# A state-space scan feeding a gated MLP: the first block's set-up, its loads and its weight preparation are ordered anew

## The chip, the cores and the metric

The kernel runs on one core of one Trainium2 chip, as one program. The metric is the device time of one execution in microseconds (us). Before the change three runs took 351.63, 351.94 and 352.17 us; the median is 351.94 us.

## The reference, cut to what matters

```python
# x [4,8,768,32], a [4,8,768], B, C [4,8,768,16]: batch, heads, sequence, width
la, cum = log(clip(a, 1e-6, 1)), cumsum(la)            # within chunks of the sequence
M  = (C @ B.T) * exp(cum_i - cum_j) * causal
y  = M @ x + (C @ state) * exp(cum)                    # inside the chunk + carried in
state = exp(sum(la)) * state + sum_j(B_j x_j * exp(cum_last - cum_j))
x  = y.transpose(0, 2, 1, 3).reshape(3072, 256)        # tokens x model width
g, val = x @ w_gate, x @ w_val                         # 256 -> 1536
return (g * sigmoid(g) * val) @ w_out                  # 1536 -> 256
```

All inputs and outputs are 32-bit floats.

## The kernel before, in words

The sequence is cut into NB = 6 blocks of 128 positions. A block holds these positions of all four batches, 512 tokens, and goes through two stages: the scan (here called attention) and the MLP.

The scan of a block works on two pieces of 64 positions. VectorE (DVE) builds the decay tile `L` with a running product (`scan_spread` in block 0, `scan_j` later): it multiplies along a row of `a` and restarts at 1 wherever the tile `dj` holds a 1, that is on the diagonal of a piece. TensorE (PE) forms the scores `S` (`scores`), DVE multiplies them by `L` (`mix`) and the keys by the decay to the piece's end (`weigh_first` in block 0, `weigh_b` later), PE forms the piece states (`sums`), the outputs `y` (`values`) and the part carried in (`carried`). `E` is the second decay tile; `ce` names the product of C with it (`weigh_c`); `apart` and `step` advance the state.

In block 0 the rows of `a` are loaded small (`load_rows`), clipped on DVE (`clip_rows`) and spread over the partitions by matmuls with a 0/1 tile (`spread`); later blocks read them back from DRAM, clipped by GpSimd (POOL) and written there once (`clip_all`, `write_all`, then `load_aj` and `load_an`).

The MLP has NF = 12 pieces f of 128 hidden units. `gate_val` makes two 128x512 products per piece, ScalarE (ACT) applies `silu`, DVE multiplies (`product`). `hid_high` and `hid_low` split the result in a rounded high part and its rest, and `project` sums three products (high-high, low-high, high-low) over all pieces. `gate_val` does the same three products in blocks 1 to 5. In block 0 it multiplies the whole 32-bit floats instead, x in the tile `xf` and the weights in `w`, which needs no low parts.

The weights arrive as 64-bit words and are made into 32-bit floats on chip, 18 pieces in all: 12 for gate and value (`wg0` to `wg11`), 6 for the projection (`wo0` to `wo5`). Piece i goes through `w_fetch` (512 KB on SP's DMA queue), `w_magnitude` and `w_rest` on ACT, `w_range` (on DVE for pieces 1 and 2, on POOL for the others), `w_shift`, `w_sign` and `w_round` on DVE. A gate piece is then ready for block 0. For the later blocks `w_high` rounds it to the tile `h`, `w_minus` writes its negative, and `w_low` adds the whole in a DMA issued by POOL, which leaves the low part `l`.

The order is written by a planner. `Plan.add` takes an engine, a cost, the steps that must come before (`needs`), the slots that a step takes and a rank; `Plan.order` plays the kernel with these costs and writes each engine's instructions in the order that comes out. An engine then executes its instructions strictly in that order. `needs` and `Plan.follow` (a list of steps that go in turn) put no wait on the chip: waits come from the data alone, and from tiles that must be free again. `lag` is the time that the planner gives a transfer on a bus that all transfers share, `slack` a margin. Tiles come from pools with a number of buffers: raw weights have 8 (`RAW`), shared with the high and low parts of the hidden values; `sg` has 21, shared by gate weights `w` and hidden values; `L`, `E`, `bc` (B and C) and `xb` (x and B by position) have one each, so that the loads of block k+1 wait for the scan of block k.

## Time and profile before

| | us |
|---|---|
| three runs: lowest, median, highest | 351.63, 351.94, 352.17 |
| profiled execution, its own time | 352.14 |
| its span | 350.3 |

The profile is of one execution. Its span is the stretch from the first to the last instruction; 1.84 us of that execution's own time lie around it. Engines are PE (matmul), PEld (weight load), DVE, ACT, POOL and SP; SPq, ACTq and POOLq are their queues where they issue DMAs. A row of a timeline has start, duration, engine, operation, written tile <- read tiles, count, and in brackets the idle time of the engine before it with what ended it. Busy PE time is 342.8 us of 350.3; the granted TensorE clock is 9 tenths or more in all 40 slices of the span.

### The profile page before, as it was taken

Reading aid. Unit: us, or ns where it says so; the run is one execution under the profiler, and the core shown is the slowest. Engines: PE = TensorE matmul, PEld = TensorE weight load, DVE = VectorE, ACT = ScalarE, POOL = GpSimd, SP = SyncE. Lnnn points to the kernel's source line nnn. Section 1 sums busy time; section 2 is a strip of 40 time slices with the busy share of each in tenths; the row PEclk is TensorE's granted clock in tenths of the full one; section 3 lists DMA queues with packets and bytes.
Section 4 is the critical chain, followed back from the end, with each engine's and each line's share of the span. In section 5 each row is a group of like instructions: output and inputs, shape, how many; then the busy total and the mean of one; then the engine's idle time right before and its main releaser. Section 6 shows DMA issues by size and latency. Waiting matters only on the chain.

```text
span 350.3 us, 7386 instructions
## 1 busy us (share of the span) xinstructions
PE 342.8 (98%) x3183; PEld 265.6 (76%) x3184; DVE 231.3 (66%) x415; ACT 121.9 (35%) x221; POOL 46.0 (13%) x36
## 2 busy tenths in 40 slices
PE   7999989999999999999999999999999999999996
PEld 5644445688878888878888878888888888888895
DVE  4999999998689774686447677456676430565320
ACT  3599677434355512212222222221212221222221
POOL 1374884402301000000000000000000000000000
PEclk9999999999999999999999999999999999999999
DMA  7799998850000751000382000281000000100001
GB/s 258 241 318 309 334 277 185 225 120 2 1 2 4 204 158 62 0 2 2 111 175 82 0 2 2 84 199 59 24 3 2 2 2 0 60 2 0 0 2 60
DMA packets 10216, 31.28 MB, mean 89 GB/s; under 512 B 1184, under 2 KB 2080, under 8 KB 9544
## 3 DMA queue, kind: packets, MB, share of 16 engines
q1 hardware_dynamic: 8136, 26.77, 25.4%
q0 software_dynamic: 1728, 3.15, 5.0%
q10 hardware_dynamic: 320, 0.89, 0.8%
q8 instruction: 25, 0.41, 0.5%
q14 instruction: 7, 0.06, 0.1%
HBM read 24.32 MB, written 3.35 MB: 79 GB/s over the span
## 4 chain that ended last, share of the span: by engine, by line
PE 92%; DVE 3%; issue 1%; ACT 0%; DVEq 0%; ACTq 0%
PE gv L191 57%; PE po L191 28%; PE y L191 5%; PE S L191 2%; DVE wg8w L191 1%; DVE L L191 1%; DVE wg0w L191 1%; DVE E L191 0%; DVE wg7w L191 0%; DVE sg L191 0%; DVE xb L191 0%; ACT ob L191 0%; DVE bc L191 0%; DVEq L191 0%; ACTq L191 0%
## 5 line engine op out<-in xcount | busy, mean ns | idle before, releaser
L191 DVE TENSOR_TENSOR sg<-gv,sg 128x512 f32<-128x512 f32 x72 | 49.5, 688 | 66.5 <-PE gv L191 65.3
L191 ACT ACTIVATE sg<-gv 128x512 f32<-128x512 f32 x72 | 43.1, 598 | 109.7 <-PE gv L191 109.6
L191 DVE TENSOR_TENSOR hh<-sg,hh 128x512 fp32r<-128x512 f32 x72 | 49.5, 691 | 16.0 <-ACT hh L191 14.6
L191 ACT CAST hh<-sg 128x512 fp32r<-128x512 f32 x36 | 22.3, 623 | 31.1 <-PE po L191 17.5
L191 DVE TENSOR_TENSOR_SCAN L<-L,dj 128x520 f32<-128x520 f32 x20 | 23.9, 1228 | 5.8 <-DMA L<-clipped 5.8
L191 ACT COPY ob<-po 128x512 f32<-128x512 f32 (+1 forms) x13 | 7.2, 555 | 48.6 <-PE po L191 48.2
L191 DVE CAST hh<-sg 128x512 fp32r<-128x512 f32 x36 | 15.8, 438 | 1.2
L191 PE MATMUL po<-hh,wo4h 128*128 128x512 f32 (+1 forms) x52 | 15.2, 375 | 0.0
L191 PE MATMUL po<-hh,wo2h 128*128 128x512 f32 (+1 forms) x52 | 15.2, 375 | 0.0
L191 PE MATMUL po<-hh,wo0h 128*128 128x512 f32 (+1 forms) x52 | 15.2, 375 | 0.0
L191 DVE TENSOR_TENSOR L<-S,L 128x512 f32<-128x512 f32 x24 | 15.1, 678 | 0.0
L191 PE MATMUL po<-hh,wo5h 128*128 128x512 f32 (+1 forms) x52 | 15.1, 373 | 0.0
L191 PE MATMUL po<-hh,wo1h 128*128 128x512 f32 (+1 forms) x52 | 15.0, 373 | 0.0
L191 PE MATMUL po<-hh,wo3h 128*128 128x512 f32 (+1 forms) x52 | 15.0, 373 | 0.0
L191 PEld LDWEIGHTS y<-L,xb 64*32 64x32 f32 x768 | 9.6, 111 | 3.1 <-issue 1.8
L191 PE MATMUL y<-L,xb 64*32 64x64 f32 x768 | 11.9, 239 | 0.0
L191 PEld LDWEIGHTS po<-hh,wo0h 128*128 128x128 f32 x52 | 9.5, 188 | 1.9 <-issue 0.2
L191 PEld LDWEIGHTS po<-hh,wo5h 128*128 128x128 f32 x52 | 9.5, 188 | 1.7
L191 PEld LDWEIGHTS po<-hh,wo1h 128*128 128x128 f32 x52 | 9.5, 188 | 1.7
L191 PEld LDWEIGHTS po<-hh,wo3h 128*128 128x128 f32 x52 | 9.5, 188 | 1.7
L191 PEld LDWEIGHTS po<-hh,wo2h 128*128 128x128 f32 x52 | 9.4, 188 | 1.8
L191 PEld LDWEIGHTS po<-hh,wo4h 128*128 128x128 f32 x52 | 9.4, 188 | 1.7
(304 smaller groups left out, 756.0 us busy)
## 6 DMA issues: line engine op xcount, KB each, us to landing
L<-clipped SPq DMA_DIRECT2D x10, 520.0 KB, 10.7
xb<-in_xb SPq DMA_DIRECT2D x5, 768.0 KB, 13.8
bc<-in_bc SPq DMA_DIRECT2D x6, 512.0 KB, 4.4
out<-ob SPq DMA_DIRECT2D x11, 256.0 KB, 2.0
E<-clipped SPq DMA_DIRECT2D x5, 260.0 KB
xb<-in_xb ACTq DMA_DIRECT2D x1, 768.0 KB, 6.3
wg0r<-in_wgv SPq DMA_DIRECT2D x1, 512.0 KB
wg1r<-in_wgv SPq DMA_DIRECT2D x1, 512.0 KB
```

Of the source, the lines that this page charges most:

```text
L191: ins = getattr(self.engine, name)(*a, **k)
```

## The change

1. `dj` is made on chip: POOL counts columns minus partitions into a new tile (`iota`, one for each piece), and DVE compares with 0. The diagonal goes out of the loaded constants `cs` (66 instead of 131 floats in a row), and ACT's copy into `dj` goes.
2. Block 0's `xb` is loaded by SP behind `bc`, no longer by ACT.
3. `w_fetch` of the projection's pieces is issued by ACT, piece 12+j in the plan behind the silu of (0, 6+j). The needs that held gate pieces 2 to 5 and 7 back go. New lists fix the order on SP: the clipped rows are written before piece 2 is fetched; then piece 8, `bc` 1, `L` 1 (`aj`), piece 9, `xb` 1, piece 10, `E` 1 (`an`), piece 11.
4. On ACT all four copies of `xf` come ahead of the preparation of pieces 2 and 3. DVE no longer makes the fourth.
5. DVE in block 0 weighs the keys before all four `mix`, and after them has E, ce, the sign and rounding of piece 0, the range of pieces 1 and 2.
6. In the plan the negative of piece i comes after the first gate product of piece i+3; the low parts' DMAs take 3.0 us of the planner's bus; the high and low parts of block 0's hidden values come after the last weight fetch. Several `lag` values are other ones, and `xh` and `xl` have slots of their own in the plan.
7. `WHOLE` = 12 and `FAR` = 0, 3..17 are new names. With NF = 12 they choose the same pieces as the conditions before did: block 0 multiplies whole floats for all 12 pieces, before and after.

```diff
-    eye, hm, blk = cs[:, 0:W], cs[:, W : W + 2], cs[:, W + 2 : W + 2 + 2 * D]
+    hm, blk = cs[:, :2], cs[:, 2 : 2 + 2 * D]
+    step_of = const.tile([P, W], F32, name="step")
...
-        (sp if k else se).dma_start(t, xb[k])
+        sp.dma_start(t, xb[k])
...
-    def w_fetch(i):
+    def w_fetch(i, e=sp):
...
-        sp.dma_start(t, src[j].bitcast(I32))
+        e.dma_start(t, src[j].bitcast(I32))
...
-        if not k:
+        if not k and f < WHOLE:
...
+    for q in range(K):
+        ge.iota(
+            step_of[piece(q)], pattern=[[1, W]], base=0, channel_multiplier=-1,
+            allow_small_or_imprecise_dtypes=True,
+        )
+    ve.tensor_scalar(dj, step_of.unsqueeze(1).to_broadcast([P, H, W]), 0.0, None, ALU.is_equal)
     ge.memset(unit[:, P:], 1.0)
     ge.memset(dn, 0.0)
...
-    add([("Act", 0.6), ("DVE", 0.6)], None, lambda e: copy(e, dj, eye.unsqueeze(1).to_broadcast([P, H, W])), -8.5, ["cs"], gives="dj")
...
-        add("SP", 0.48, do(w_fetch, i), r - 9.0, [("S", 0, BATCH - 1)] if i in (2, 3) else [("M", 0, 2 * i - 7)] if i in (4, 5) else [("y", 0)] if i == 7 else [], takes=[("raw", ("raw", i))], gives=("raw", i), lag=2.1)
+        if i < NF:
+            add("SP", 0.48, do(w_fetch, i), r - 9.0, takes=[("raw", ("raw", i))], gives=("raw", i), lag=1.3)
+        else:
+            add("Act", 0.4, do(w_fetch, i, se), due(0, i - LAST), [("si", 0, i - LAST)], takes=[("raw", ("raw", i))], gives=("raw", i), lag=1.3)
...
-            add("Act", 0.57, do(w_minus, i), r - 2.6, [("round", i), ("gv", 0, 0, 0)], gives=("minus", i))
-            add("Pool", 1.2, do(w_low, i), r - 2.5, [("wh", i), ("minus", i), *whole_done], uses=[("w", i)], gives=("wl", i), slack=4.0)
+            add("Act", 0.57, do(w_minus, i), r - 2.6, [("round", i), ("gv", 0, min(i + 3, NF - 1), 0)], gives=("minus", i))
+            add("Pool", 1.2, do(w_low, i), r - 2.5, [("wh", i), ("minus", i), *whole_done], uses=[("w", i)], gives=("wl", i), lag=3.0)
...
-    add("SP", 0.48, write_all, -9, ["clipped"], gives="written", lag=0.9)
+    add("SP", 0.48, write_all, -9, ["clipped"], gives="written", lag=4.2)
...
-                add([("Act", 0.36)] if i < 3 else [("Act", 0.36), ("DVE", 0.36)], None, do(x_whole, i), -1 + i / 10, [("vals", i) if i < 2 else ("y", 0), "xf", *([("round", 0)] if i == 3 else [])], uses=[y[i]], gives=("xf", i))
+                add([("Act", 0.36)], None, do(x_whole, i), -1 + i / 10, [("vals", i) if i < 2 else ("y", 0), "xf"], uses=[y[i]], gives=("xf", i))
...
-            add([("Act", 0.6), ("DVE", 0.36)], None, do(hid_high, k, f), r, [("pr", k, f)], takes=[("raw", h)], uses=[t], gives=("hh", k, f))
+            add([("Act", 0.6), ("DVE", 0.36)], None, do(hid_high, k, f), r, [("pr", k, f), *([] if k else [("raw", NW - 1)])], takes=[("raw", h)], uses=[t], gives=("hh", k, f))
...
-    plan.follow([("L", 0, b) if i else ("scan0", b) for b, i in halves] + [("M", 0, p) for p in range(3)] + [("bt", 0)] + [("M", 0, 3), ("E", 0), ("ce", 0), ("sign", 0)])
+    for steps in ORDER:
+        plan.follow(steps)
+    plan.follow([("L", 0, b) if i else ("scan0", b) for b, i in halves] + [("bt", 0)] + [("M", 0, p) for p in range(NP)] + [("E", 0), ("ce", 0), ("sign", 0), ("round", 0), ("range", 1), ("range", 2)])
...
-CST = W + 2 + 2 * D
+CST = 2 + 2 * D
...
+WHOLE = 12
+LAST = 6
+FAR = [0, *range(3, 18)]
 PAGE = 4.4
+ORDER = (
+    ["written", ("raw", 2)],
+    [("raw", 8), ("bc", 1), ("aj", 1), ("raw", 9), ("xb", 1), ("raw", 10), ("an", 1), ("raw", 11)],
+    [("xf", 3), ("mag", 2), ("rest", 2), ("mag", 3)],
+    [("y", 0), ("xf", 2)],
+)
```

## Rows read from the trace of the kernel before

**Rows 1.** Part 1 of the page: busy us of each engine, share of the span, instructions.

```profile
PE 342.8 (98%) x3183; PEld 265.6 (76%) x3184; DVE 231.3 (66%) x415; ACT 121.9 (35%) x221; POOL 46.0 (13%) x36
```

**Rows 2.** The waits of PE in the whole span: waiting tile <- what ended the wait: us in total, times, longest.

```profile
PE a L191 <- DVE rows L191: 1.4, 1, 1.4
PE gv L191 <- DVE wg8w L191: 1.2, 1, 1.2
PE rest L191 <- DVE warm L191: 1.1, 1, 1.1
PE gv L191 <- DVE wg0w L191: 0.4, 1, 0.4
```

**Rows 3.** The chain of work that ended last, in order of time: start, us, what.

```profile
16.75 0.14 issue
16.89 20.84 PE gv L191 x48
...
46.94 0.14 issue
47.08 3.67 PE gv L191 x8
```

**Rows 4.** The timeline of the first 17 us: POOL, DVE and ACT.

```profile
1.09 0.71 POOL L191 MEMSET dn<- 128x520 f32 x2
...
3.46 0.86 DVE L191 TENSOR_SCALAR rows<-rows 8x512 f32<-8x512 f32 x2 [2.45 <-DMA rows<-in_aj]
...
5.07 0.63 ACT L191 COPY dj<-cs 128x520 f32<-128x520 f32 x1 [1.03 <-DMA cs<-in_cst]
5.72 1.88 DVE L191 TENSOR_TENSOR_SCAN L<-a,dj 128x260 f32<-128x260 f32 x3 [1.40 <-ACT dj L191]
6.34 1.34 ACT L191 ACTIVATE Cz<-bc,cs 128x512 f32<-128x512 f32 x2 [0.64 <-DMA bc<-in_bc]
...
7.70 3.04 DVE L191 TENSOR_TENSOR_SCAN L<-a,dj 128x260 f32<-128x260 f32 x5
...
10.67 1.85 DVE L191 TENSOR_TENSOR L<-S,L 128x512 f32<-128x512 f32 x3
...
10.85 1.92 POOL L191 TENSOR_SCALAR wg0w<-wg0w 128x512 f32<-128x512 f32 x1 [0.40 <-ACT wg0w L191]
...
16.66 0.42 DVE L191 COPY xf<-y 128x256 f32<-128x256 f32 x1
```

**Rows 5.** The timeline of PE from 4.30 to 4.45 us: the matmuls of the first spread, which run in it.

```profile
3.93 1.25 PE L191 MATMUL a<-rows,pick 8*128 8x260 f32 x2 [1.40 <-DVE rows L191]
```

**Rows 6.** The timeline of PE: the scores of block 0.

```profile
8.13 2.30 PE L191 MATMUL S<-Cz,bc 32*64 32x128 f32 x64
```

**Rows 7.** Issues of DMAs from the page (KB each, median us from issue to landing): the two that ACT issues.

```profile
xb<-in_xb ACTq DMA_DIRECT2D x1, 768.0 KB, 6.3
...
cs<-in_cst ACTq DMA_DIRECT2D x1, 65.5 KB, 3.4
```

**Rows 8.** The timeline of SP's DMA issues, and as last line the time to landing of `wg8r`.

```profile
16.70 1.15 SPq L191 DMA_DIRECT2D L<-clipped  x2
...
19.20 0.43 SPq L191 DMA_DIRECT2D xb<-in_xb  x1
19.96 0.33 SPq L191 DMA_DIRECT2D wg8r<-in_wgv  x1
...
DMA to landing us min/median/max: 16.8/16.8/16.8
```

**Rows 9.** The timeline from 32 to 50 us: what DVE, ACT, POOL and PE do around the wait for `wg8w`.

```profile
37.06 0.66 ACT L191 ACTIVATE wg8w<-wg8r 128x512 f32<-128x512 f32 x1
...
38.27 3.18 POOL L191 TENSOR_SCALAR wg8w<-wg8w 128x512 f32<-128x512 f32 x1
...
41.62 1.22 DVE L191 TENSOR_TENSOR_SCAN E<-E,dn 128x520 f32<-128x520 f32 x1
42.77 0.66 DVE L191 TENSOR_TENSOR L<-S,L 128x512 f32<-128x512 f32 x1
43.35 0.77 DVE L191 TENSOR_SCALAR wg8w<-wg8w 128x512 int32<-128x512 int32 x1
...
45.24 1.09 DVE L191 TENSOR_TENSOR bc<-bc,E 128x512 f32<-128x512 f32 x1
...
42.33 3.60 PE L191 MATMUL gv<-xf,wg7w 128*128 128x512 f32 x8
47.08 3.67 PE L191 MATMUL gv<-xf,wg8w 128*128 128x512 f32 x8 [1.15 <-DVE wg8w L191]
```

**Rows 10.** Busy time by stretch: us of the stretch, then PE busy (count), PEld, DVE, ACT, POOL, granted clock, DMA share, GB/s.

```profile
15.00:20.00 5.00, 4.60 (x56) 2.41 (x42) 4.79 (x10) 4.99 (x12) 1.05 (x1) 1.00 1.02 406
...
45.00:50.00 5.00, 3.85 (x10) 1.53 (x9) 5.00 (x9) 3.38 (x7) 3.84 (x3) 1.00 1.09 294
...
60.00:100.00 40.00, 40.00 (x226) 31.00 (x225) 33.84 (x59) 15.98 (x29) 9.43 (x6) 1.00 0.32 80
```

**Rows 11.** The timeline of POOL and PE: the first and the last low part, and the first matmul that reads one.

```profile
27.94 1.03 POOL L191 DMA_DIRECT2D wg0l<-wg0w  x1
...
65.26 0.62 PE L191 MATMUL gv<-xh,wg0l 128*128 128x512 f32 x2
...
68.34 1.18 POOL L191 DMA_DIRECT2D wg11l<-wg11w  x1
```

More of the change, by code (lines that the diff above doesn't have):

```diff
@@ L587, in w_low @@
         hi = part[i]["hi"]
-        if i < NF:
+        if i < WHOLE:
             lo = part[i]["lo"]
@@ L666, in idle @@
             rest[n] = ps_at.tile([P, 512], F32, tag="at", name=f"rest{n}")
-        times, wide = (4, 64) if not n else (1, 512)
+        times, wide = ((4, 64), (1, 512))[n]
         for _ in range(times):
@@ L733, in scan_moe_kernel @@
         add("DVE", 0.6, do(w_round, i), r - 3.3, [("sign", i), ("rest", i)], uses=[("raw", i)], gives=("round", i))
-        if i < NF:
+        if i < WHOLE:
             r = due(1, i) - LATER
@@ L737, in scan_moe_kernel @@
         whole_done = [("gv", 0, i, m) for m in range(2)]
[L738 to L740 removed]
+        if i < WHOLE:
+            add("Act", 0.57, do(w_minus, i), r - 2.6, [("round", i), ("gv", 0, min(i + 3, NF - 1), 0)], gives=("minus", i))
+            add("Pool", 1.2, do(w_low, i), r - 2.5, [("wh", i), ("minus", i), *whole_done], uses=[("w", i)], gives=("wl", i), lag=3.0)
         else:
@@ L765, in load @@
             return do(f, k) if k else lambda: None
-        add(*q, load(load_bc), FETCH["bc"] if k == 1 else z - 7 if k else -7.7, late + behind("bc") + loaded, takes=[("bc", BC)], gives=("bc", k), lag=2.1)
-        add(*q, load(load_xb), FETCH["xb"] if k == 1 else z - 6 if k else -6, late + behind("xb") + loaded, takes=[("xb", XB)], gives=("xb", k), lag=3.1)
+        add(*q, load(load_bc), FETCH["bc"] if k == 1 else z - 7 if k else -7.7, late + behind("bc") + loaded, takes=[("bc", BC)], gives=("bc", k), lag=1.3)
+        add(*q, load(load_xb), FETCH["xb"] if k == 1 else z - 6 if k else -6, late + behind("xb") + loaded, takes=[("xb", XB)], gives=("xb", k), lag=2.6)
         if not k:
-            add("-", 0.0, lambda: None, -9, takes=[("x", "rows")], gives="rows", lag=0.2)
+            add("-", 0.0, lambda: None, -9, takes=[("xl", "rows")], gives="rows", lag=0.2)
             for i in range(3):
@@ L777, in scan_moe_kernel @@
                     add("PE", 0.25 if first(b, i) else 0.45, do(spread, b, i), r + 0.5 * i, [("clip", b % 2 if b < BATCH else 2), "pick"], takes=[("mm" if first(b, i) else "at", t)], uses=[t, "rows"], gives=t, kind="s")
-                    need = [t, ("decays", 0), "dj"] + ([("scan0", b)] if i else [])
+                    need = [t, ("decays", 0)] + ([("scan0", b)] if i else [])
                     done = ("E", 0) if b == BATCH else ("L", 0, b) if i else ("scan0", b)
@@ L782, in scan_moe_kernel @@
             add("SP", 0.96, do(load_aj, k), FETCH["aj"] if k == 1 else z - 12, ["written", ("decays", k), *late], gives=("aj", k), lag=4.3)
-            add("SP", 0.48, do(load_an, k), FETCH["an"] if k == 1 else z - 9, ["written", ("decays", k), *late], gives=("an", k), lag=1.1)
+            add("SP", 0.48, do(load_an, k), FETCH["an"] if k == 1 else z - 9, ["written", ("decays", k), *late], gives=("an", k), lag=2.4)
             for b in range(BATCH):
@@ L846, in scan_moe_kernel @@
             c = 1.4
-            if not k:
+            x = [("xh", k), ("xl", k)]
+            if not k and f < WHOLE:
                 need = [("round", f), *(("xf", i) for i in range(2 * K))]
                 c = 1.72
+                x = ["xf"]
             gv = [("gv", k, f, m) for m in range(2)]
             for m in range(2):
-                add("PE", c, do(gate_val, k, f, m), r + m * 0.1, need, takes=[("mm", gv[m])], uses=[gv[m], ("x", k) if k else "xf"], gives=gv[m], kind="r")
+                add("PE", c, do(gate_val, k, f, m), r + m * 0.1, need, takes=[("mm", gv[m])], uses=[gv[m], *x], gives=gv[m], kind="r")
             t = ("sg", k, f)
```

18 lines of the change are left out of this document (8 added, 10 removed).

## The prediction

> **What bounds the kernel now.** I read the busy times first, then what PE waited for, then the chain of waits, and last the timelines of the stretches that the change touches. PE is busy for 342.8 of 350.3 us [rows 1]. Of the 7.5 us left, four waits are named: 1.1 us for the first memset, 1.4 us for the clipped rows, 0.4 us for the first rounded weight piece and 1.2 us for piece 8 [rows 2]; the rest is mostly the last copy and store, which the change leaves alone. In the chain, DVE's work sets the start: the first gate matmul begins at 16.89 us, just behind the rounding of `wg0w`. Then PE leads, but for the one gap that ends at 47.08 us with the rounding of `wg8w` [rows 3]. From 60 to 100 us PE is busy in all 40 us, with the granted clock at 1.00 [rows 10]. So only two things can pay: an earlier first gate matmul, and the gap at 47 us. What the change does elsewhere can only cost.
>
> **The diagonal on chip.** The first running product starts at 5.72 us, after 1.40 us in which DVE waited for ACT's copy of `dj`; the rows were clipped by 3.46 + 0.86 = 4.32 us [rows 4]. With `dj` there early, what is late next is the first spread: its two matmuls run from 3.93 to 3.93 + 1.25 = 5.18 us [rows 5]. So the start moves from 5.72 to 5.18, a gain of 0.54; if a scan can start right behind the clipped rows it is 1.40, and it isn't less than nothing while `dj` is ready by 5.18. I take 0.54, since the spread's end is in a row.
>
> The trace has no `iota` and no such comparison. The two `iota` stand ahead of POOL's memsets, of which the two that fill 520 columns took 0.71 us together; POOL's longest plain pass over 512 columns at the start is 1.92 us [rows 4]. So two passes over 65 columns cost between some tenths of a us and 3.8 us; I take the memsets as the nearest rows, 0.7. The comparison writes 520 columns: on DVE between 0.42, a copy of 256 [rows 4], and 1.22, a scan of 520 [rows 9]; I take the shift of 512, 0.77 [rows 9]. From POOL's start near 1.1 us that gives about 1.1 + 0.7 + 0.8 = 2.6 us, and DVE waits until 3.46 for the rows anyway: cost nothing. In the worst case, 1.1 + 3.8 + 1.22 = 6.1 us, DVE's queue holds the clipping behind it, and the start is 6.1 + 0.86 - 4.32 = 2.6 us later than now.
>
> **The rest of DVE's opening.** From 5.72 to 16.75 us DVE runs almost without a pause: eight scans, a clipping, four `mix`, the keys, E, ce, three steps on piece 0. The new order moves the keys in front and removes none, so the chain keeps its length and is carried 0.54 earlier, if nothing else turns late. The scores end at 8.13 + 2.30 = 10.43 us [rows 6]; the scans would end near 10.2, the keys fill 0.6, and the first `mix` stands at 10.8 instead of being held by the scores. The copies of `xf` need the last `y`, which profits from the keys coming early; the fourth, 0.42 us on DVE at 16.66 [rows 4], goes to ACT where one takes about as long, and the gate's first half doesn't read it. This also frees 0.42 us of DVE. Sum for the start: 0.54.
>
> **xb on SP's queue.** ACT's load of it took 6.3 us to land [rows 7]; issued behind `bc` it goes out a few tenths later, and the keys need it only at 10.2. Between 15 and 20 us, with one queue in use, the DMA engines are full at 406 GB/s [rows 10], so one queue is no bottleneck. [...]
>
> `cs` gets narrower. It landed 3.4 us after its issue [rows 7], and the first to need it is now the scaling of C, at 6.34 us [rows 4], 1.3 us after the copy of `dj` could read it: there is that slack. [...]
>
> **The gap at 47 us.** `wg8r` was issued at 19.96 and took 16.8 us, to 36.8; it stood on SP's queue behind `L` and `xb` of block 1 [rows 8]. ACT read it at 37.06, POOL took 3.18 us for its range to 41.45, and DVE's three steps on it were mixed with E, a `mix` and ce of block 1, so PE stood for 1.15 us [rows 9]. The new order puts pieces 7 and 8 ahead of all of block 1: 2 x 520 + 768 + 512 KB less in front, 2.3 MB, at 406 GB/s 5.7 us and at 294 GB/s 7.9 us [rows 10]. Piece 8 lands at 29 to 31 us, 6 to 8 us earlier, and DVE has it ready ahead of work whose result PE needs later. DVE is busy 5.00 of 5 us there [rows 10], so the step is only an exchange: E, one `mix` and ce, 1.22 + 0.66 + 1.09 = 2.97 us [rows 9], must go behind the rounding of piece 8. PE needs that 0.54 + 1.15 us earlier than now; DVE gives 0.54 + 0.42 + up to 2.97. It is enough, but only where the planner places it so. Gain 1.15, between 0 (the gap moves to piece 9 or 10) and 1.15.
>
> **Moves priced at nothing.** Block 1's `L`, `E` and `xb` land later by two pieces, 1 MB, under 4 us at the rates above; DVE has weights to round in the meantime. Low parts go later: now the first is issued at 27.94, read at 65.26, the last issued at 68.34 [rows 11]; the first has 37 us of cover. If the cover were gone, block 1's gate would wait for POOL's queue. The hidden values' high and low parts of block 0 move behind the last fetch; DVE is busy 33.84 of 40 us from 60 to 100 and ACT 15.98 [rows 10], which holds them. `WHOLE` and `FAR` choose what was chosen before: nothing. The spare slots of `xh` and `xl` change the plan, no work.
>
> **Sum.** 352.14 (the profiled execution's own time, 350.3 of it the span) - 0.54 - 1.15 = 350.45; that execution stood 0.20 above the median of 351.94, so 350.25 us, shown as 350.2.
>
> **Rivals.**
> - *More at the start.* The scan follows the clipped rows at once: 1.40 instead of 0.54, with the gap closed, 352.14 - 1.40 - 1.15 - 0.20 = 349.4. For it: the wait named in [rows 4] ends with `dj`. Against: the end of the first spread [rows 5].
> - *The gap moves.* DVE is full until 60 us, and a wait at piece 9 or 10 takes the place of that at 8: 352.14 - 0.54 - 0.20 = 351.4. [...]
> - *POOL's queue, slower.* Low parts are issued later and share POOL with the ranges, in strict order. If the low part of piece i stands in front of the range of piece i+4, that range waits for ACT's negative, which stands behind the silu of piece i+2 or i+3. After half a gate piece (1.8 of 3.60 us [rows 9]) come the negative (0.66 as ACT's pass in [rows 9]), the issue (1.03 [rows 11]), the range (1.92 [rows 4]) and DVE's three steps (0.66 to 0.77 each [rows 9], 2.1): 7.5 us, where PE arrives after 3.6. Each such place costs 3.9 us: 350.25 + 3.9 = 354.1 with one. For it: POOL already took 3.18 us for a range beside low parts. Against: the plan gives low parts a late rank. It decides as soon as one range stands so.
> - *Nothing at all.* `dj` is late by the slow `iota` and eats what the gap returns: 352.14 + 2.6 - 1.15 - 0.20 = 353.4, also slower.
>
> **How the numbers follow.** The forecast has 0.52, its own range 349.7 to 350.9; more at the start 0.13; the gap moved, or `cs` late, 0.20; POOL's queue 0.11; the slow `iota` 0.04. A measurement of this kernel can tell about 0.2%, 0.7 us, from no change, that is 351.24 to 352.64. Faster: 0.52 + 0.13 = 0.65. Same: 0.20. Slower: 0.11 + 0.04 = 0.15. The range from 349.0 to 352.2 takes in the first three cases and leaves the slower ones out.
>
> **What would show it.** Right: the first scan of `L` near 5.2 us with PE's `a` as what ended the wait; the first gate matmul near 16.35; `wg8r` landing before 31 us; no wait of PE for a `wg` tile; all later stages as long as now. Wrong: a wait of DVE for POOL's `step`, a wait of PE for `wg9w` or `wg10w`, a range on POOL behind a low part with PE idle 4 us after, or PE idle between 60 and 120 us. The prediction falls if the time is above 351.2 or under 349.

## The result, and the profile after

The changed kernel took 355.79 us in the median of 5 runs (354.24 to 356.43), the kernel before beside it 351.94 (351.63 to 352.56): ratio 1.0093, 95% interval [1.007, 1.0116]. Run again with the first experiments it took 354.3 (353.45 to 359.47, 6 runs) against 351.87, ratio 1.005 [1.0031, 1.0068]. The ratios come from the fast executions alone, without that of 359.47 us, so they aren't the quotients of the medians. By the medians the change is slower by 2.4 to 3.9 us; I had forecast 1.7 us faster.

The profiled execution took 354.24 us, its span 352.2, so 1.9 us longer than before. Part 1 of its page:

```profile
PE 343.4 (97%) x3184; PEld 265.6 (75%) x3184; DVE 229.6 (65%) x413; ACT 122.5 (35%) x223; POOL 48.4 (14%) x38
```

PE is busy for 343.4 us instead of 342.8 [rows 1], with the same products; so some 1.3 of the 1.9 us are idle time. PE's waits in the changed kernel (columns as in [rows 2]):

```profile
PE a L191 <- DVE rows L191: 1.4, 1, 1.4
PE po L191 <- issue: 1.4, 1, 1.4
PE gv L191 <- issue: 1.3, 1, 1.3
PE rest L191 <- DVE warm L191: 1.1, 1, 1.1
PE y L191 <- DVE bc L191: 0.2, 1, 0.2
```

The waits for `wg8w` (1.2 us) and `wg0w` (0.4) are gone, as forecast. In their place stand two with no releaser, "issue". Where they lie is seen in the chain of waits after the change:

```profile
15.11 1.13 PE y L191 x32
16.24 0.90 PE rest L191 x2
17.14 20.60 PE gv L191 x48
37.73 1.14 PE S L191 x63
38.87 10.60 PE gv L191 x24
49.47 1.64 PE y L191 x106
51.11 1.05 PE gv L191 x2
52.16 1.30 issue
53.47 4.45 PE gv L191 x10
57.92 1.88 PE y L191 x117
...
98.94 5.89 PE po L191 x24
104.83 1.41 PE y L191 x91
106.25 1.37 issue
107.61 5.73 PE po L191 x24
113.35 1.88 PE y L191 x117
```

And the same places in the chain of the kernel before, which [rows 3] had cut out:

```profile
37.73 1.23 PE S L191 x63
...
50.75 1.64 PE y L191 x105
52.39 5.35 PE gv L191 x12
57.73 1.88 PE y L191 x117
...
104.42 1.41 PE y L191 x91
105.83 5.67 PE po L191 x24
111.50 1.88 PE y L191 x117
```

Read the starts side by side. The scores of block 1 start at 37.73 in both: the start gave nothing in this profile. The first `y` of block 1 starts 1.28 us earlier (49.47 for 50.75): the gap is closed. The second `y` is 0.19 later: 1.30 us of idle time in the middle of gate piece 9. In block 2 the first `y` is 0.41 late and the second 1.85, 1.37 of it idle time in the middle of a projection. After that nothing changes.

The steps of the start, in the timeline of the changed kernel:

```profile
0.85 0.42 POOL L191 IOTA step<- 64x65 f32 x2 [0.40 <-POOLq L955]
1.30 0.73 DVE L191 TENSOR_SCALAR dj<-step 128x520 f32<-128x520 f32 x1 [0.29 <-POOL step L191]
5.20 1.88 DVE L191 TENSOR_TENSOR_SCAN L<-a,dj 128x260 f32<-128x260 f32 x3 [0.88 <-PE a L191]
10.24 1.07 DVE L191 TENSOR_TENSOR xb<-xb,L 128x512 f32<-128x512 f32 x1
11.24 2.47 DVE L191 TENSOR_TENSOR L<-S,L 128x512 f32<-128x512 f32 x4
15.71 0.69 DVE L191 CUSTOM_DVE_ANT_0 wg0w<-wg0r,wg0w 128x1024 uint16<-128x1024 uint16 x1
```

The first scan starts at 5.20 us behind the first spread, where [rows 4] have 5.72. `wg0w` is rounded at 16.40 instead of 16.74, but the gate doesn't follow: `y`, two `rest` products (nothing reads their result) and the copies of `xf` hold it to 17.14 in the chain above (16.97 in the timeline, 16.89 before).

**What an "issue" of this length is.** Part 3 of the page of the changed kernel has a queue that no line of the kernel issues:

```profile
q8 instruction: 25, 0.41, 0.5%
```

25 transfers of 16 KB. That they are PE's instructions, in pages, is inferred: the 6368 products and weight loads over 25 pages are 255 each. The trace's records of these transfers give each page's start and duration; none tells when a page is asked for, and where an expectation below says "requested", the time beside it is the start of the transfer. In block 2 of the changed kernel one starts at 105.18 us and takes 1.07. The DMA view of that stretch (105.1 to 105.3 us) holds this transfer alone:

```profile
DMA packets 1, 0.02 MB, mean 82 GB/s; under 512 B 0, under 2 KB 0, under 8 KB 0
## 3 DMA queue, kind: packets, MB, share of 16 engines
q8 instruction: 1, 0.02, 33.3%
```

It ends at 106.25, where PE's idle time begins, and PE goes on at 107.61. In the kernel before the same page started at 101.36, 3 us ahead of `y`. In block 1 the page starts at 51.24 us and ends at 52.21; PE stands from 52.16 to 53.47. In all such stretches of the profiles below, seventeen, PE goes on 1.1 to 1.5 us behind the end of a page. `y` is a run of small products, 256 instructions with the weight loads in 1.5 to 1.7 us; a page took 0.9 us or more and PE went on 1.1 us or more behind it. From these numbers I estimate that `y` uses up a page (255 instructions) faster than the next one comes, and that the page has to be under way about when `y` starts.

PE's weight loads (PEld) of the changed kernel show what stood in front in block 2: a load of the projection waited for the low part of a hidden value, 1.1 us before the page started.

```profile
104.10 0.19 PEld L191 LDWEIGHTS po<-hh,wo1h 128*128 128x128 f32 x1 [0.34 <-DVE hh L191]
```

### The profile page after: what moved, and what is told of

Same layout as the page of the kernel before. It is cut to its first block, busy times and chain, and to the rows that moved or that the text cites. A ratio compares the mean times of both kernels' runs of the same rounds, so it can differ in the third digit from the quotient of the medians.

```text
span 352.2 us, 7395 instructions
## 1 busy us (share of the span) xinstructions
PE 343.4 (97%) x3184; PEld 265.6 (75%) x3184; DVE 229.6 (65%) x413; ACT 122.5 (35%) x223; POOL 48.4 (14%) x38
## 4 chain that ended last, share of the span: by engine, by line
PE 94%; issue 1%; DVE 1%; ACT 0%; ACTq 0%
PE gv L191 59%; PE po L191 28%; PE y L191 5%; PE S L191 2%; PE rest L191 0%; DVE E L191 0%; DVE L L191 0%; DVE bc L191 0%; ACT ob L191 0%; DVE wg0w L191 0%; ACTq L191 0%
## 5 line engine op out<-in xcount | busy, mean ns | idle before, releaser
L191 DVE TENSOR_TENSOR hh<-sg,hh 128x512 fp32r<-128x512 f32 x72 | 49.5, 691 | 15.8 <-ACT hh L191 14.2
L191 DVE TENSOR_TENSOR_SCAN L<-L,dj 128x520 f32<-128x520 f32 x20 | 24.9, 1269 | 10.3 <-DMA L<-clipped 10.3
L191 ACT CAST hh<-sg 128x512 fp32r<-128x512 f32 x32 | 19.9, 622 | 24.6 <-PE po L191 16.5
L191 DVE CAST hh<-sg 128x512 fp32r<-128x512 f32 x40 | 17.1, 427 | 2.4 <-PE po L191 1.2
```

Of the source, the lines that this page charges most:

```text
L191: ins = getattr(self.engine, name)(*a, **k)
```

## The experiments

My theory from this profile: a wait in PE's queue that costs PE nothing by itself holds back the next page. In block 2 that is a late hidden value, in block 1 the late fourth `mix`. Four runs on one chip first.

**e1_again**: the changed kernel once more.

> The changed kernel once more, to see the times spread and a second profile. Theory (late page): PE gets its instructions in pages of 16 KB; the request for the next page goes out only when PE's queue has passed the wait in front of it, so a wait that costs PE nothing by itself delays the page, and the scan's small matmuls then use up what is left before it lands. It expects the two idle stretches of PE named issue, 1.3 us behind the first y of block 1 and 1.4 us behind the first y of block 2, in every profile, and in an execution of 356 us a third place or a longer one of the same kind, about 2 us. Rival (transfers): ACT's weight loads and the late low parts hold up the instruction transfers; it expects the first stretch to vary with the DMA traffic and the second, where nothing is transferred, to be something else.

354.3 us, ratio 1.005 [1.0031, 1.0068]; both stretches again, 0.5 and 1.8 us. The pages start at 50.14 and 104.41.

**e2_mix_first**: all mixes of block 1 ahead of the sign of piece 9.

```diff
     [("y", 0), ("xf", 2)],
+    [("M", 1, NP - 1), ("sign", 9)],
```

> One list more: the four products of scores and decay of block 1 come ahead of the sign step of piece 9 on DVE. In the changed kernel the last of them ends at 50.18 us and the page is requested 1.06 us after that. Theory (late page): with the products done about 1.2 us earlier the page comes about 1.2 us earlier, the wait of 1.30 us behind the first y of block 1 shrinks to 0.3 us or less, the one in block 2 stays; time 1 to 1.3 us below the changed kernel. Rival (transfers): the wait behind y of block 1 stays within 0.3 us of 1.30, since the transfers are the same.

353.62, ratio 1.0039 [1.0013, 1.0066]. No idle stretch in block 1, but PE waited 1.4 us for `wg8w` again, so this alone decides nothing; block 2's stretch is there (1.3), inside `y` this time.

**e3_hh_free**: the hidden values of block 0 don't stand behind the last fetch.

```diff
-            add([("Act", 0.6), ("DVE", 0.36)], None, do(hid_high, k, f), r, [("pr", k, f), *([] if k else [("raw", NW - 1)])], takes=[("raw", h)], uses=[t], gives=("hh", k, f))
+            add([("Act", 0.6), ("DVE", 0.36)], None, do(hid_high, k, f), r, [("pr", k, f)], takes=[("raw", h)], uses=[t], gives=("hh", k, f))
```

> Only the new need of the hidden values' high parts in block 0 (the last weight fetch) is taken back. In the changed kernel the low part of the fourth hidden piece ends at 104.05 us, PE's queue waits for it, and the page is requested 1.13 us after. Theory (late page): these parts come earlier, the page of block 2 is requested before the scan starts, the wait of 1.37 us behind the first y of block 2 goes; the one of block 1 stays: 1.4 to 1.6 us below the changed kernel. Rival (the order of PE's instructions puts a page's end at a bad place): the order on PE is the same, so the wait stays.

353.74, ratio 1.0044 [1.0026, 1.0063]. Block 2's page starts at 102.34 and its stretch is gone. The time didn't follow: PE now waits 1.8 us for a silu, since ACT stands in front of a fetched projection piece (timeline of ACT in this kernel):

```profile
74.28 0.65 ACT L191 ACTIVATE wo4r<-wo4r 128x512 int32<-128x512 uint32 x1 [5.58 <-DMA wo4r<-in_wo]
```

**e4_mix_hh**: both edits.

> Both edits together. Theory (late page): both waits named issue go or fall under 0.3 us each; the profiled execution is 2.4 to 2.9 us below that of the changed kernel, near 351.5 us and so at the kernel before, and the spread of the runs falls under 1 us. Rival (transfers): one wait or both stay, 353 us or more.

352.7, ratio 1.0011 [0.9994, 1.0027]: 1.6 us of the loss is back by the medians, not all of it as expected, and its runs spread over 2.9 us. Block 2 is clean, page at 102.04. Left are 1.1 us for `wg8w` and 0.6 of "issue" in block 1. DVE in this kernel stood for `bc` of block 1, which the new order sends behind pieces 7 and 8:

```profile
28.61 1.33 DVE L191 TENSOR_SCALAR Cz<-bc,cs 128x512 f32<-128x512 f32 x2 [1.69 <-DMA bc<-in_bc]
```

**e5_cz_act**: e4, and the scaling of C of blocks 0 and 1 on ACT alone.

```diff
-        add([("Act", 1.35), ("DVE", 0.72)], None, do(heads_apart, k), z, [("bc", k)], takes=[("Cz", CZ)], gives=("Cz", k))
+        add([("Act", 1.35)] if k < 2 else [("Act", 1.35), ("DVE", 0.72)], None, do(heads_apart, k), z, [("bc", k)], takes=[("Cz", CZ)], gives=("Cz", k))
```

> The changed kernel with both edits of the last run (hidden values free to go early, all four mixes of block 1 ahead of the sign of piece 9), and in addition the scaling of C of block 1 (Cz) only on ACT, as in the kernel before. Theory: what is left of the loss after those two edits is DVE held by a load that the new order puts behind pieces 7 and 8: the wait of Cz for bc was 1.7 us in the last run, and PE then waited 1.1 us for wg8w. With Cz on ACT DVE has no wait for bc, PE's wait for wg8w falls under 0.4 us, and the time comes to 351.3 to 352.0 us, ratio 0.998 to 1.000. Rival (the wait for bc hides nothing; wg8w is late because DVE has too much work before it): the wait for wg8w stays at 1 us or more and the time at 352.5 to 353.

352.58, ratio 1.0024 [1.0008, 1.004]. The wait for `wg8w` went, as the theory said, and the time stayed above what it said: ACT now stands 1.56 us for `wg9r`, and PE 1.7 us for the silu behind it. The wait for a load had only changed its engine.

**e6_dj_alone**: the kernel before with the diagonal on chip, and only that.

```diff
+    step_of = const.tile([P, W], F32, name="step")
...
+    for q in range(K):
+        ge.iota(
+            step_of[piece(q)], pattern=[[1, W]], base=0, channel_multiplier=-1,
+            allow_small_or_imprecise_dtypes=True,
+        )
+    ve.tensor_scalar(dj, step_of.unsqueeze(1).to_broadcast([P, H, W]), 0.0, None, ALU.is_equal)
...
-    add([("Act", 0.6), ("DVE", 0.6)], None, lambda e: copy(e, dj, eye.unsqueeze(1).to_broadcast([P, H, W])), -8.5, ["cs"], gives="dj")
...
-                    need = [t, ("decays", 0), "dj"] + ([("scan0", b)] if i else [])
+                    need = [t, ("decays", 0)] + ([("scan0", b)] if i else [])
```

> The kernel before with one part of the change alone: the diagonal made on chip by POOL and DVE; the loads and all else as before. Theory of the prediction: the first scan starts 0.5 us earlier and the whole start with it; the first gate matmul near 16.4 and the time near 351.4 us, ratio 0.9985. Rival (the start is held by a second chain, the last y, its copies and the two idle matmul groups on PE, which stood at the same time in the changed kernel): the first scan is early, the first gate matmul stays within 0.2 us of 16.9, and the time within 0.2 us of the kernel before.

351.53 against 352.08, ratio 0.9977 [0.9966, 0.9987]; first gate matmul at 16.16.

**e7_late_mix**: the kernel before with one mix of block 1 behind the rounding of piece 9.

```diff
+    plan.follow([("round", 9), ("M", 1, 0)])
```

> The kernel before with one mix of block 1 (that of batch 0) put behind the rounding of piece 9 on DVE; it then ends near 50.4 us instead of 42.8 to 43.4, before PE has finished piece 8 at 50.75, so PE doesn't wait for its data. Theory (PE's instructions are fetched in pages; the request for the next page stands behind the wait in PE's own queue, so a mix that is late, yet not late enough to be waited for, makes the page late): the page that came at 50.39 us comes between 51.2 and 51.8, and PE shows an idle stretch with no releaser of 0.5 to 1.5 us in piece 9 or 10; time 0.5 to 1.5 us above the kernel before. Rival (the page is late because of the DMA traffic of the new order of loads, which this kernel doesn't have): page at 50.4, no such stretch, and the time within 0.3 us of the kernel before.

352.46, ratio 1.0006 [0.9988, 1.0024] (the profile is of its highest time, 354.26). The page came at 51.32, inside my range, but `y` had started only at 51.17 and there was no idle stretch. The page came 0.08 us behind the mix's end (51.24); in e3 it came ahead of the fourth mix's end (50.34 for a page at 50.00). In block 2 the page started 1.1 us behind the wait in front of it; had a mix held the page back here, it should come as far behind the mix. So the mix half of my theory falls.

**e8_old_loads**: e4 with the old order of the loads around block 1.

```diff
-    [("raw", 8), ("bc", 1), ("aj", 1), ("raw", 9), ("xb", 1), ("raw", 10), ("an", 1), ("raw", 11)],
+    [("raw", 6), ("bc", 1), ("aj", 1), ("raw", 7), ("xb", 1), ("raw", 8), ("an", 1), ("raw", 9)],
```

> The changed kernel with the hidden values free to go early, the mixes of block 1 ahead of the sign of piece 9, and the order of the loads around block 1 as the kernel before had it (bc and L behind piece 6, xb behind piece 7, E behind piece 8). Theory (the new order of the loads is itself a part of the loss, by DVE's wait for bc): DVE has no wait for bc over 0.3 us, L lands earlier, and the time is at or below 352.0 us, about that of the run with Cz on ACT. Rival (the order of loads is neutral or better than the old one): the gap before wg8w comes back at 1 us or more as in the kernel before, and the time is 352.7 or above.

351.34 against 352.08, ratio 0.9986 [0.9965, 1.0007]: by the two ratios the load order is worth 0.9 us on top of e4, but the two intervals overlap, so that this is likely and not shown. Neither `wg8w` nor `wg9r` holds anything; the scaling of C is on ACT again. PE's waits in this kernel behind the start:

```profile
PE gv L191 <- issue: 0.5, 1, 0.5
PE gv L191 <- ACT sg L191: 0.4, 1, 0.4
```

**e9_product_first**: e8 with DVE's product of gate piece 6 ahead of the mixes. In the changed kernel, a load in piece 8 waited for it.

```diff
+    [("round", 8), ("pr", 0, 6), ("shift", 9), ("M", 1, 0), ("M", 1, 1), ("M", 1, 2), ("M", 1, 3), ("sign", 9)],
+    [("pr", 0, 6), ("shift", 10)],
+    *([("pr", 0, 6), ("hl", 0, f)] for f in range(1, 6)),
```

> The kernel of the last run (old order of the loads around block 1, hidden values early, mixes early), and in addition DVE makes the product of the gate piece (0, 6) right behind the rounding of piece 8, ahead of the mixes of block 1. Seen before it: in the changed kernel and in each variant whose page came late in block 1, one weight load of PE in piece 8 waits 0.25 to 0.36 us for DVE's product of piece 6, which frees a half of the accumulators, and the page starts 2.8 to 4.0 us behind that wait; in the two kernels whose page was in time no load waits for that product. Theory: this short wait holds the front of PE's queue and so the request. With the product early, no weight load of piece 8 waits for DVE's product, the page starts no later than 0.5 us behind the start of y of block 1, and the idle stretch in piece 9 (0.45 us in the last run) is gone; time 350.8 to 351.2 us. Rival (the late page has nothing to do with the wait): page again 0.9 us or more behind the start of y, idle stretch 0.4 us or more, time as the last run, 351.3.

351.71, ratio 0.9991 [0.9977, 1.0004] (one of its twelve runs took 430.15 us, at a mean granted clock of 0.76; why it was so low isn't known). No load waited for the product any more, and the page still came 0.67 us behind the start of `y`. This wait isn't the cause either. PE stood 0.5 us for a page in the second `y` of block 1 instead.

**e10_quiet** and **e16_quiet_again**: the changed kernel without the low parts' transfers and with later fetches of the projection's weights; one profile each.

```diff
-            ge.dma_start(lo, part[i]["w"].bitcast(F32), accum_op=ALU.add)
+            pass
...
-            add("Act", 0.4, do(w_fetch, i, se), due(0, i - LAST), [("si", 0, i - LAST)], takes=[("raw", ("raw", i))], gives=("raw", i), lag=1.3)
+            add("Act", 0.4, do(w_fetch, i, se), due(0, min(i - 3, NF - 1)), [("si", 0, min(i - 3, NF - 1))], takes=[("raw", ("raw", i))], gives=("raw", i), lag=1.3)
```

> The changed kernel without the transfers that run beside block 1's scan: the 12 low parts of the gate weights aren't added (so the output lacks them), and the projection's pieces are fetched from the silu of piece 9 on instead of 6. DVE's order through block 1 is that of the changed kernel. Theory 1 (the request is late because of a wait in PE's queue, and on its way it is delayed by other transfers): the wait for DVE's product near 47.2 us is there again, the page starts 1.0 to 1.6 us behind it, as in block 2 where no other transfer ran (1.08 us), and there is no idle stretch in piece 9. Theory 2 (traffic plays no part): the page starts 2.8 us or more behind that wait, 0.9 us or more behind the start of y, and PE idles 0.4 to 1.3 us in piece 9.

> The quiet kernel a second time, since the page of block 1 came 0.96 us and 1.84 us behind y in two profiles of the changed kernel: if the quiet run shows a cause and not a scatter, the page again starts within 0.3 us of the start of y and piece 9 has no idle stretch; if it was scatter, the page may be 0.9 us behind.

The page starts 0.15 us ahead of `y`, and 0.36 behind it the second time; the idle stretch in piece 9 is gone, and 0.2 us. Theory 2 falls: what was taken away matters. Theory 1 missed its own number: the load that waits for DVE's product does so until 46.06 us, and the page starts 2.1 us behind it, not 1.0 to 1.6. The single executions took 350.32 and 350.99 us.

**e14_no_low** and **e15_wo_late**: one of the two edits each.

> The changed kernel without the transfers of the 12 low parts (the output lacks them), with the projection's fetches where the change has them. Two things were taken away in the quiet run; this takes one. If the low parts' transfers delay the page of block 1: page within 0.3 us of the start of y (-0.22 in the quiet run), no idle stretch in piece 9. If it is the projection's fetches: page 0.9 us or more behind, idle stretch 0.4 us or more.

> The changed kernel with the projection's weights fetched from the silu of piece 9 on, not 6, and the low parts as the change has them. If the projection's fetches delay the page of block 1: page within 0.3 us of the start of y, no idle stretch in piece 9. If it is the low parts' transfers: page 0.9 us or more behind, idle stretch 0.4 us or more. In either case the hidden values come later still, so block 2's idle stretch stays.

Without the low parts' transfers the page starts 0.15 us behind `y`, without an idle stretch; with them and with late fetches 1.54 us behind, with 1.2 us of idle time. So it is the low parts, though POOL's issue of them goes with the transfers here, and the two aren't told apart. In both, the hidden values stay behind the last fetch and block 2 keeps its stretch (1.3 and 0.4). The single executions took 352.38 and 359.94 us. In that of e15 DVE stood 5.7 us for a later `xb`, and PE 3.8 us for DVE, to 86.95; from 85.9 to 92.7 us the granted clock was 0.50.

**e17_late_low**: e8 with all low parts, those of pieces 2 to 11 moved behind the first `y` of block 1.

```diff
-            add("Act", 0.57, do(w_minus, i), r - 2.6, [("round", i), ("gv", 0, min(i + 3, NF - 1), 0)], gives=("minus", i))
+            add("Act", 0.57, do(w_minus, i), r - 2.6, [("round", i), ("gv", 0, max(min(i + 3, NF - 1), 9 if i > 1 else 0), 0)], gives=("minus", i))
```

> The changed kernel with the old order of the loads around block 1, the hidden values early and the mixes early (the run that came to 351.34), and in addition the negatives of pieces 2 to 11 stand on ACT behind the silu of piece 9, so that no low part's transfer runs beside the first y of block 1. Theory (low parts' transfers delay PE's page in block 1): the page starts within 0.5 us of y, the idle stretch in piece 9 is under 0.1 us (0.45 without this edit), and the time is 350.7 to 351.2 us. Rival (the projection's fetches, which now run alone there, or something else delays it): the page is 0.9 us or more behind y, the stretch 0.4 us or more, the time 351.3 or above.

The page comes 0.49 us ahead of `y` and the stretch is gone, as the theory said. The DMA view from 48.5 to 52.4 us of this kernel shows how quiet it is:

```profile
DMA packets 1, 0.02 MB, mean 4 GB/s; under 512 B 0, under 2 KB 0, under 8 KB 0
## 3 DMA queue, kind: packets, MB, share of 16 engines
q8 instruction: 1, 0.02, 1.5%
```

But the time is 357.66, ratio 1.0164 [1.0127, 1.0202]. I had moved the low parts too far; among PE's waits in this kernel:

```profile
PE gv L191 <- DMA wg2l<-wg2w: 3.5, 1, 3.5
PE gv L191 <- DVE sg L191: 1.9, 2, 1.3
```

The longest wait ends at 73.82 us. Behind it the granted clock falls: from 74.6 to 78.0 us it is 0.51, and two products in a row take 1.05 us there that took 0.62 before. If the fall comes from the wait, which is inferred, the wait cost more than its own length (columns as in [rows 10]):

```profile
70.00:74.50 4.50, 0.95 (x5) 0.59 (x4) 0.62 (x1) 0.00 (x0) 0.17 (x1) 1.00 1.11 197
74.60:78.00 3.40, 3.40 (x9) 2.61 (x8) 0.00 (x0) 0.60 (x1) 1.33 (x3) 0.51 1.10 257
```

**e11_wo_sp**: the changed kernel with the projection's weights fetched by SP.

> The changed kernel with one part undone: the projection's weights are fetched by SP again, behind the last gate piece, not by ACT one by one. In the plan the last fetch then comes earlier, and so do the hidden values of block 0. Theory (block 2's idle stretch comes from hidden values that are late because they stand behind the last fetch): the idle stretch of 1.4 us behind the first y of block 2 goes, that in block 1 stays, time 352.6 to 353.2 us. Rival (ACT's issue of these loads costs nothing and the hidden values are late for another reason): time as the changed kernel, 354.3 or above, the stretch in block 2 is there.

353.68, ratio 1.004 [1.0018, 1.0061]. Block 2's stretch is gone, as expected (page at 101.98); the time is under the changed kernel's 354.3 by less than I said, and its runs spread from 350.82 to 355.23.

**e12_loads_alone**: the changed kernel with the old order of the loads.

> The changed kernel with one part undone: the order of the loads around block 1 is that of the kernel before (bc and L behind piece 6, xb behind piece 7, E behind piece 8). Theory (the load order costs by itself about what it cost between the runs with and without it, 0.9 us): 353.2 to 353.6 us, with the idle stretch of block 2 still there. Rival (what the old order gives shows only together with the other two edits, since each closes a gap that the next one waits in): 354 us or above.

354.28, ratio 1.0067 [1.0045, 1.009]: the rival. By itself the old order gives nothing that shows; both stretches are there (1.3 each). `wg8r` is read only at 35.53 us here, and PE doesn't wait for `wg8w` all the same.

**e13_start_parts**: e6, with the other steps of the start (keys first, copies of `xf` on ACT, range of pieces 1 and 2 later).

```diff
-                add([("Act", 0.36)] if i < 3 else [("Act", 0.36), ("DVE", 0.36)], None, do(x_whole, i), -1 + i / 10, [("vals", i) if i < 2 else ("y", 0), "xf", *([("round", 0)] if i == 3 else [])], uses=[y[i]], gives=("xf", i))
+                add([("Act", 0.36)], None, do(x_whole, i), -1 + i / 10, [("vals", i) if i < 2 else ("y", 0), "xf"], uses=[y[i]], gives=("xf", i))
...
-    plan.follow([("L", 0, b) if i else ("scan0", b) for b, i in halves] + [("M", 0, p) for p in range(3)] + [("bt", 0)] + [("M", 0, 3), ("E", 0), ("ce", 0), ("sign", 0)])
+    plan.follow([("xf", 3), ("mag", 2), ("rest", 2), ("mag", 3)])
+    plan.follow([("y", 0), ("xf", 2)])
+    plan.follow([("L", 0, b) if i else ("scan0", b) for b, i in halves] + [("bt", 0)] + [("M", 0, p) for p in range(NP)] + [("E", 0), ("ce", 0), ("sign", 0), ("round", 0), ("range", 1), ("range", 2)])
```

> The kernel before with those parts of the change alone that lie in its first 17 us: the diagonal made on chip, the keys weighed ahead of the mixes, the range of pieces 1 and 2 behind piece 0, all four copies of xf on ACT ahead of pieces 2 and 3. All loads, the projection's weights, the low parts and the hidden values stay as before. Theory (the start's part of the prediction was right and was hidden in the changed kernel by what came later): first gate matmul 0.7 to 1.1 us earlier than in the kernel before, no idle stretch behind y in block 2, the gap before wg8w still there; time 351.0 to 351.4 us. Rival (the start gains nothing, as the one profile of the changed kernel shows): first gate matmul at 16.6 or later, time 351.8 or above.

352.15 against 352.0, ratio 1.0016 [0.9999, 1.0032]. The first gate matmul is at 16.33, 0.56 earlier, but the wait for piece 8 takes it back (PE's waits in this kernel; 1.2 in [rows 2]):

```profile
PE gv L191 <- DVE wg8w L191: 1.6, 1, 1.6
```

DVE works without a pause ahead of it and has piece 8 rounded at 46.77 us, only 0.16 earlier than before (46.93). In e6 and e18, which have the same loads and the first gate matmul 0.73 and 0.59 earlier, it is rounded at 46.07 and 46.02 and the wait is 1.0 and 0.8 us. So it isn't the load that takes the gain back, but DVE's work ahead of the rounding.

**e18_dj_again**: e6 a second time.

> The kernel before with the diagonal made on chip and nothing else, a second time, on one chip with the run beside it. If this part alone gives what was measured first: 351.3 to 351.7 us where the kernel before takes 352.0, ratio 0.997 to 0.999. If the first time was a scatter: ratio 0.9995 or above.

351.59 against 351.88, ratio 0.9994 [0.9973, 1.0015]: the gain of 0.55 us was 0.3 this time and can't be told from none.

**The pages together.** Start of block 1's page against the first product of `y`, and whether PE stood in piece 9:

| kernel | y | page | page - y | idle, "issue" |
|---|---|---|---|---|
| before | 50.68 | 50.39 | -0.29 | none |
| e18, e5, e13, e7 | 49.76 to 51.17 | 49.06 to 51.32 | -0.70, 0.10, 0.13, 0.15 | none |
| changed, two profiles | 49.40, 49.18 | 51.24, 50.14 | 1.84, 0.96 | 1.3, 0.5 |
| e12 (its page took 1.6 us), e15 | 48.87, 49.86 | 50.20, 51.40 | 1.33, 1.54 | 1.3, 1.2 |
| e4, e8 | 50.46, 48.87 | 51.39, 49.81 | 0.93, 0.94 | 0.6, 0.5 |
| e6 | 49.82 | 50.34 | 0.52 | none |
| e11 (its page took 1.8 us) | 49.94 | 50.40 | 0.46 | 0.6 |
| e2, e9, e3 | 50.22, 49.00, 48.89 | 50.89, 49.67, 50.00 | 0.67, 0.67, 1.11 | none; PE waits 0.2 to 0.6 us for `wg9w` or a mix instead |
| no low part under way: e17, e10, e14, e16 | 48.30 to 49.57 | 48.15 to 49.65 | -0.49, -0.15, 0.15, 0.36 | 0, 0, 0, 0.2 |

The idle time follows the lateness of the page with some 0.3 to 0.5 us of grace, and less where the page itself took longer (e11, e12). The four profiles without a low part under way have the page in time; e14 is the weakest of them, since PE also stood 1.1 us for `wg8w` before `y`. But a low part under way isn't enough to make the page late: e5 has the changed order and low parts there, and its page is in time. So are, but for e6 (0.52 behind, no stretch), the pages of the kernels ordered as before, in which low parts and SP's loads run beside `y` too. In those PE stands 0.8 to 1.6 us for `wg8w` just ahead of `y`, but that doesn't explain them: in e2, e4 and e15 it stands 1.1 to 1.5 us there as well, and their pages come 0.67 to 1.54 us behind `y`, while e5 has no such wait. What else is needed stays open.

Block 2 sorts without exception, if e17 is left aside, whose block 1 lost over 5 us. In the eight profiles with the hidden values behind ACT's last fetch (changed, e1, e2, e10, e12, e14 to e16) the page starts from 0.45 us before `y` to 0.88 behind it and PE stands 0.4 to 1.8 us; in the eleven others it starts 2.6 to 4.0 us ahead and PE doesn't stand. In each of the eight a load of the projection waits 0.10 to 0.45 us for a hidden value, and the page starts 1.0 to 1.8 us behind that wait with no other transfer in between; in the eleven no load waits for one in the 5 us ahead of the page. So the order of events is the same in all nineteen; that the wait itself delays the page is inferred.

## Why the prediction was wrong

**The diagonal on chip: right at its place, and only there.** The two `iota` took 0.42 us together where I had 0.7, the comparison 0.73 where I had 0.77; `dj` was ready at 2.03, the first scan started at 5.20 (5.18 forecast), with PE's `a` as what ended the wait. Alone it gave 0.55 and then 0.3 us by the medians (e6, e18), where I had 0.54; the second interval includes no gain. The slow `iota` falls. The late `cs`, which the chances name beside the moved gap, no run shows: it landed 3.0 us after its issue (3.4 in [rows 7]; over all profiles with a landing 2.5 to 3.7 for the narrow rows and 2.5 to 3.9 for the wide ones), and the scaling of C stood 2.04 us for `bc`, not for it. "More at the start" falls by the 5.20.

**The rest of DVE's opening: right in kind, not in size.** The keys took 1.07 us instead of 0.6, so the first `mix` stood at 11.24 and not 10.8 (in most of the variants they took 0.69), and E at 13.63, no earlier than before (13.65). That the gain reaches the gate held in most profiles (first gate matmul at 15.8 to 16.7 in sixteen of the eighteen with an early diagonal; 16.89 and, in e7, 17.29 without) and not in the two of the changed kernel itself (16.97, 16.85). There the chain runs over the 32 products of `y` carried in, which take 1.13 us where others take 0.69 (last section), over two `rest` products and the `xf` copies. e13 shows a second limit that I had not priced: an earlier gate gains nothing until DVE's work ahead of piece 8 moves with it.

**xb on SP's queue.** It landed 5.2 us after its issue (6.3 before) and held nothing. ACT's six fetches of the projection's pieces have no term in the sum; their issues took 0.33 to 0.37 us each, and what they carried with them cost time (below).

**The gap at 47 us: closed as forecast, but not by the load.** `wg8r` was read at 24.62 us, even earlier than my 29 to 31 (timeline of the changed kernel):

```profile
16.43 0.33 SPq L191 DMA_DIRECT2D wg8r<-in_wgv  x1
...
24.62 0.69 ACT L191 ACTIVATE wg8w<-wg8r 128x512 f32<-128x512 f32 x1
```

PE's wait went, and `y` came 1.28 us earlier for a forecast of 1.15. But the earlier load isn't what closes the gap. DVE starts on piece 8 at 41.39 us, 10 us behind its range, and ends at 45.65, with all four mixes of block 1 behind it and E and ce still ahead. e8, e9, e12 and e17 have the old order of the loads, `wg8r` read at 35.5 to 36.1, and no wait for `wg8w`; of the ten others with the new order six wait for it again (0.4 to 1.5 us). What decides is when DVE comes to its three steps. At the start of the kernel I had asked "what is late next"; I didn't ask it here, and it is PE's instructions: their page came at 51.24 us, 1.84 behind the first product of `y`. The new order also gave the wait a second way back, `bc` of block 1, on DVE in e2 to e4 and as `wg9r` on ACT in e5.

**Moves priced at nothing: the step that failed.** "The hidden values' high and low parts of block 0 move behind the last fetch; DVE is busy 33.84 of 40 us from 60 to 100 and ACT 15.98 [rows 10], which holds them": they fit in the engines' time, but the planner then wrote them into the projection's own time. PE's load waited 0.34 us for one of them, the page for the small products of block 2 started 1.1 us behind that, and PE stood 1.37 us. Taking that one need away removes the stretch (e3, e4), and so does another way to earlier hidden values (e11). "Low parts go later ... the first has 37 us of cover": true for who reads them, but PE's page for block 1 comes up to 1.84 us behind `y` (1.3 us of idle time), and in time in each profile without low parts beside it. I had asked only who waits for a low part, not what its transfer or its issue does to others. My rival on POOL's queue had the right sign and the wrong mechanism: no range held PE, and that its 354.1 lies near the 354.24 of this profile is luck. What late low parts can cost is seen in e17, where PE waits 3.5 us for one.

**The sum.** By the starts in the two chains: start 0.00 (-0.54 forecast), gap -1.28 (-1.15), page of block 1 with the `y` and gate around it +1.47, block 2's projection +0.22, its page and what is around it +1.44, together +1.85, the difference of the spans. 350.25 was thus missed by the 0.54 that didn't reach the gate in this profile and by 3.1 us of which the text had none, less 0.1 that the gap gave more; the other 0.4 us to 354.24 are the 0.20 that I had taken off and 0.25 outside the span. The medians lie up to 1.55 us above this profile's 354.24; that part isn't explained. Of the wide spread of the variants two forms are seen: a landing late under ACT or DVE (e3, e5, e15), and a lower clock. In e2, e5, e8, e12, e13 and e18 the highest time, 1.6 to 4.1 us above the median, is the one with a mean granted clock of 0.994 or 0.995, where the others have 0.998 or more; in e17's profile, at 0.995 too, a wait of 3.55 us stands ahead of the fall.

**What is settled.** Shown: block 2's stretch comes from the hidden values' new place. Block 1's is gone in all four profiles without low parts beside it; that they are needed rests on these four, and they aren't enough by themselves (e5 and the kernels ordered as before). Likely, not shown: the new load order costs 0.9 us once block 2 is clean and the mixes are early (e4 and e8). Open: why a page starts late behind a wait in the one case, what makes it late in the other, what the medians have above the profile, and whether any version beats the kernel before by a margin. e8 at 351.34 and the diagonal alone at 351.53 and 351.59 are the lowest medians, and of their three intervals only one excludes no gain.

## What to carry to other kernels

A gap that ends with one engine's result also covers everything else that arrives at its own time; before you close it, look for the next arrival, and in a stretch of many small instructions the instructions themselves can be one (here a page that started 1.84 us behind `y`). An edit that only moves work off the critical path still moves its transfers and what waits for it: read where it lands, not only whether the engine has room. And a single undo can show nothing while a second loss takes its place: three edits that gave 0.7 us or less each alone, which none of these runs can tell from nothing, gave over 2 us together.

## What the runs showed of the hardware

- The transfers of 16 KB that I take for PE's instructions (25 in the changed kernel) took 0.9 us to 2.2 us (most about 1.0), and in all seventeen stretches where PE stood behind one it went on 1.1 to 1.5 us behind its end. In the waits these stretches are an "issue" of 0.2 to 1.8 us in the middle of a row of like products.
- Where no other transfer ran, a page started 1.0 to 1.8 us behind the wait in front of it (block 2, eight profiles).
- In two profiles the granted clock fell to 0.5 at a long wait of PE: for 3.4 us, from 0.8 us behind the end of a wait of 3.55 us (e17), and for 6.8 us, from the last us of a wait of 3.81 us (e15). That the waits are the cause isn't shown.
- The 32 products of `y` carried into block 0 took 0.69 to 1.13 us, and differ even between two profiles of one kernel (e6 0.69, e18 1.13). The trace's clock records begin at 1.00 only between 13.9 and 17.0 us (15.90 before, 16.93 in the changed kernel); for the time ahead the trace holds no record, and the views print 1.00 there. The duration sorts by that moment: 0.69 in the six profiles where it lies ahead of these products, 1.13 in the eight where it lies at their end or later, 0.75 to 1.02 in the six where it falls among them. What the clock was before its first record isn't shown.
